# Start ticks of weight conversions in an FFT filter followed by two MLPs

## Chip, cores and metric

The kernel runs on one core of a Trainium2 chip. The metric is the device time of one execution in microseconds (us); a run is repeated, and the median counts.

## What is computed

```python
def _attn_ref(x, filt_r, filt_i):            # x: (2, 3008, 256)
    X = np.fft.rfft(x, axis=1)
    Y = X * (filt_r + 1j * filt_i)[None]
    return np.fft.irfft(Y, n=x.shape[1], axis=1)

def _moe_ref(x, w_in, w_out):                # x: (6016, 256), w_in: (256, 2048), w_out: (2048, 256)
    h = x @ w_in
    return np.maximum(0.01 * h, h) @ w_out

def _moe2_ref(x, w_in, w_out):
    r = np.maximum(x @ w_in, 0.0)
    return (r * r) @ w_out
```

The output is `_moe2_ref(_moe_ref(_attn_ref(x)))`, each MLP with weights of its own, all in float32.

## The kernel before, in words

The Fourier transform comes first, as products with small constant matrices on TensorE; it fills the first 130 us. Then come the two MLPs. Everything below is about them.

**Tiles and steps.** The 6016 tokens are cut into six macro tiles, 0 to 5, of 2 x 512 or (tiles 2 and 5) 2 x 480 tokens. The 2048 hidden units are cut into eight pairs of 128, p = 0 to 7. One step is one pair for one macro tile: 45 matmuls, 21 of them up (line 368, results `ph`, weights `wai` or `wbi`), 24 of them down (line 463, sums `py`, weights `wao` or `wbo`). The up product is a Strassen scheme: seven block products instead of eight, from blocks `b11`, `b21`, `b22` of the tile and from sums `t1` to `t4` of blocks. In the first MLP tile 0 is visited with pairs 0 to 3, then tile 1 with all pairs, then tile 0 again with pairs 4 to 7, then tiles 2 to 5; the second MLP visits tiles 0 to 5. That is 96 steps.

**Two-part numbers.** A float32 product is made of three matmuls of rounded parts: each operand is split into a rounded part `hi` (a ScalarE copy, line 338 for a tile, 269 for weights) and the rest `lo` (a subtraction on VectorE or GpSimd, line 344 for a tile, 273 for weights). The tile's seven operands are called `xop`; their sums `xs` are made at line 333 on GpSimd.

**Inside a step.** `up` (lines 408 to 449) has four parts. The first makes two products, and VectorE's `v` (line 402). The second makes three, of which the last adds into the buffer that `v` has read, and VectorE's `u` and an `h`. The third makes none. The fourth makes two, of which the first adds into the buffer that `u` has read, and two more `h`. For each of four results ScalarE makes `g` and `gp` (lines 381, 382), and GpSimd their difference (line 391). `down` (line 451) follows `up` of the next step, part by part. At the end of a tile `finish` copies the sums `py` out, on VectorE and ScalarE (lines 485 to 489).

**Ticks.** What is not part of a step is set by a clock that goes on by 8 ticks (`TM`) per step. `begin` puts the entries of a table (name of a piece of work: ticks from its start) on a list, and `tick` issues what is due. Engines take their instructions in the order in which they are issued, so the tables decide what stands ahead of what on each engine. A tick is 1.3 us where a step is 10.5 us. Tile 1 begins at tick 32, the second visit of tile 0 at 96, tiles 2 to 5 at 128, 192, 256 and 320, and the second MLP at 384. The preparation of a tile (`MACRO`) goes from 24 ticks before its beginning to 2 after it.

**Weights.** They arrive as 64-bit floats and are made into 32-bit ones by `narrow_w` (lines 193 to 257): ScalarE takes the absolute value (`size`, line 209), VectorE makes two passes (`upper`, lines 213 and 214), then one each for `signed` (217), `exp` (222) and `low` (228), and `add` (236) puts the parts together, first for half 0 (the up weights, `wi`), then for half 1 (the down weights, `wo`). `sums` (241 to 244) makes four more blocks on GpSimd. The first MLP's pairs 4 to 7 go through table `NARROW_1`, with start ticks `STARTS_1`, and are split at once. The second MLP's eight pairs go through `NARROW_2`, from tick `STARTS_2` on, one every 32 ticks, and are put to DRAM; `split_w` loads and splits them later (`SPLIT_W`, table start 8 ticks per pair, and `LATE`). The raw words are `wraw`, loaded on SyncE's queue; each load waits for `low` of the pair before. All other loads and stores are on SyncE's queue too.

The two tables as they stand:

```python
NARROW_2 = dict(
    size0=4, upper0=7, signed0=7, exp0=9, low0=10, load0=10, size1=10, add0=12, upper1=15, signed1=15, sums=16, exp1=16,
    low1=17, load1=17, add1=18, out_o=19, out_i=26,
)
MACRO = dict(
    load=-24, sum0=-16, sum1=-15, sum2=-12, hi_b11=-11, sum3=-9, hi_b21=-8, hi_t2=-8, lo_b11=-8, lo_t2=-8,
    hi_t1=-7, hi_t4=-7, lo_t1=-7, lo_b21=-6, hi_t3=-2, lo_t3=-1, lo_t4=0, hi_b22=1, lo_b22=2,
)
```

Of the kernel before, what the change touches and what calls it, by code (L numbers as in the profile page):

```python
# [30 lines left out]
NP = DFF // (2 * P)  # L31
TT = 512
NWA = 4
# [27 lines left out]

TM = 8
STARTS = (-10, 34, 72, 112)
STARTS_1 = (0, 16, 32, 56)
STARTS_2 = 80


HALF = 4
# [13 lines left out]
    low1=17, load1=17, add1=18, out_o=19, out_i=26,  # L82
)

LATE = 20
SPLIT_W = dict(load=16, hi_i=18, hi_o=19, lo_i=20, lo_o=23)
FIRST = dict(
    hi_t1=-13, hi_b11=-13, lo_t1=-13, lo_b11=-13, sum1=-12, hi_b21=-12, lo_b21=-11, hi_t2=-11, lo_t2=-10, sum2=-9,
# [14 lines left out]
    S=("lo_o",),  # L103
    M=("lo_b11", "lo_b21", "lo_t2", "lo_t3", "lo_t4"),
# [47 lines left out]
def fft_filter_then_two_mlps(  # L152
# [102 lines left out]
    def split_w(layer, p, kind, w):  # L255

        t = {}

        def load():
            for k, (n, tag) in enumerate(((7, "wi32"), (4, "wo32"))):  # L260
                w[k] = wt_p.tile([P, n, P], F32, tag=tag, name=tag, bufs=1)
                nc.sync.dma_start(w[k], w2_d[p][:, 7 * k : 7 + 4 * k])

        def hi(k):
            pool, tag = (wa_p, "wa") if p < NWA else (wb_p[0], "wb")
            n = (7, 4)[k]
            t[k] = pool.tile([P, 2, n, P], F32R, tag=tag + "io"[k], name=tag + "io"[k])
            (w_in, w_out)[k][layer, p] = t[k]
            nc.scalar.activation(t[k][:, 0], w[k], AF.Copy)

        def lo(k):
            eng = engine(kind, "lo_" + "io"[k])
            eng.tensor_tensor(t[k][:, 1], w[k], t[k][:, 0].bitcast(F32), ALU.subtract)

        return {
            "load": load, "hi_i": lambda: hi(0), "hi_o": lambda: hi(1), "lo_i": lambda: lo(0), "lo_o": lambda: lo(1),
        }

    def engine(kind, step):
        return nc.vector if step in ON_VECTOR[kind] else nc.gpsimd  # L280
# [4 lines left out]
    def begin(c, steps, table, start):  # L285

        due[c].extend((start + t, steps[name]) for name, t in table.items())
# [12 lines left out]
    NM = len(macros)  # L300
# [195 lines left out]
    with ExitStack() as fctx:  # L496
# [268 lines left out]
        for p in range(NWA, NP):  # L765
            begin("M", narrow_w(0, p, "N1"), NARROW_1, STARTS_1[p - NWA])
        for p in range(NP):
            begin("M", narrow_w(1, p, "N2"), NARROW_2, STARTS_2 + 4 * p * TM)
            begin("M", split_w(1, p, "S", {}), SPLIT_W, ((NM - 1) * NP + p) * TM + (LATE if p >= NWA - 1 else 0))
        for part in range(4):  # L770
            up(0, part)
        up(1, 0)
# [6 lines left out]
    for i in range(last):  # L779
        v, p = steps[i]  # L780
        l, m, _, p1 = visits[v]
        accs = dict(acc)
        if (i + 1) * TM == STARTS_2:
            for k in range(2):
# [64 lines left out]
```

## Time and profile before

| | |
|---|---|
| median of 3 runs | 1163.13 us (1162.51 to 1165.67) |
| profiled execution, its own time | 1165.77 us |
| its span | 1163.1 us |
| TensorE (PE) busy | 1117.3 us, 96% |
| weight loads (PEld) busy | 883.9 us |
| GpSimd (POOL) busy | 765.6 us, 66% |
| VectorE (DVE) busy | 652.8 us, 56% |
| ScalarE (ACT) busy | 649.8 us, 56% |
| TensorE's waits for VectorE's `u`, all | 15.7 us in 8 |
| TensorE's waits for VectorE's `v`, all | 11.6 us in 5 |
| GpSimd's subtraction for an activation (line 391) | 1318 ns on average, 384 of them |
| mean granted clock of TensorE | 0.993 |

How to read it: the span goes from the first to the last instruction of the profiled execution. PE, DVE, ACT, POOL and SP are TensorE, VectorE, ScalarE, GpSimd and SyncE. A row of the timeline gives an instruction's start and length, and in brackets the idle time of its engine just before it and what ended that. The granted clock is the share of full speed that TensorE was given.

### The profile page before, as it was taken

How to read it: one execution, taken by the hardware profiler on the slowest of the kernel's cores; microseconds unless marked ns; L12 is line 12 of the kernel's file. 1: busy time of each engine (PE TensorE's matmuls, PEld its weight loads, DVE VectorE, ACT ScalarE, POOL GpSimd, SP SyncE). 2: the span in 40 equal slices, each digit the busy share in tenths (PEclk: the TensorE clock that was granted, in tenths of full speed). 3: DMA queues.
4: the chain of work that ended last, by engine and by line, in shares of the span. 5: the costliest groups of instructions: out<-in, count | busy, mean ns of one | idle time of the engine just before them, and what ended most of it. 6: DMA issues, size and time to landing. Idle time of an engine off the chain costs nothing.

```text
span 1163.1 us, 14072 instructions
## 1 busy us (share of the span) xinstructions
PE 1117.3 (96%) x4800; PEld 883.9 (76%) x4800; DVE 652.8 (56%) x870; ACT 649.8 (56%) x1209; POOL 765.6 (66%) x616
## 2 busy tenths in 40 slices
PE   7899978999899899899899999999999999999998
PEld 3466866888688688678688788788888788788887
DVE  6899788565854854855744643533534434435432
ACT  3855456554554554555555765655656555656554
POOL 3785598777757857756767876745647547557544
PEclk9999999999999999999999999999999999999999
DMA  7653712116022022023032030010100200200100
GB/s 229 189 158 117 265 54 78 55 56 239 20 82 95 23 84 86 19 80 96 1 111 87 28 106 38 31 40 1 63 11 1 71 1 1 71 1 1 37 1 34
DMA packets 35238, 80.12 MB, mean 69 GB/s; under 512 B 4544, under 2 KB 14880, under 8 KB 35040
## 3 DMA queue, kind: packets, MB, share of 16 engines
q1 hardware_dynamic: 35168, 79.25, 20.6%
q8 instruction: 37, 0.61, 0.2%
q14 instruction: 33, 0.27, 0.1%
HBM read 51.31 MB, written 27.92 MB: 68 GB/s over the span
## 4 chain that ended last, share of the span: by engine, by line
PE 76%; DVE 10%; ACT 4%; issue 4%; POOL 3%; DMA 2%; SPq 0%; DVEq 0%; POOLq 0%; ACTq 0%
PE py L463 38%; PE ph L368 34%; DVE xop L344 3%; PE pi L629 1%; POOL gp L391 1%; ACT g L381 1%; PE pa L571 1%; PE px L583 1%; DMA xin<-in_x 1%; ACT xop L338 1%; DVE u L402 1%; DVE wm L213 1%; DVE wi L222 1%; PE zps L613 1%; ACT gp L382 1%
## 5 line engine op out<-in xcount | busy, mean ns | idle before, releaser
L391 POOL TENSOR_TENSOR gp<-g,gp 128x512 fp32r<-128x512 f32 (+1 forms) x384 | 502.6, 1318 | 340.0 <-ACT gp L382 102.4
L463 PE MATMUL py<-gp,wao 128*128 128x512 f32 (+1 forms) x1152 | 287.8, 391 | 0.3 <-POOL gp L391 0.3
L463 PE MATMUL py<-gp,wbo 128*128 128x512 f32 (+1 forms) x1152 | 288.0, 392 | 0.0
L368 PE MATMUL ph<-xop,wai 128*128 128x512 f32 (+1 forms) x1008 | 259.2, 394 | 20.5 <-DVE v L402 11.6
L368 PE MATMUL ph<-xop,wbi 128*128 128x512 f32 (+1 forms) x1008 | 254.9, 391 | 8.7 <-DVE u L402 8.7
L463 PEld LDWEIGHTS py<-gp,wbo 128*128 128x128 f32 x1152 | 217.2, 189 | 48.1 <-POOL gp L391 0.2
L463 PEld LDWEIGHTS py<-gp,wao 128*128 128x128 f32 x1152 | 216.5, 188 | 48.5 <-POOL gp L391 0.7
L368 PEld LDWEIGHTS ph<-xop,wai 128*128 128x128 f32 x1008 | 187.7, 188 | 69.3 <-DVE v L402 14.1
L368 PEld LDWEIGHTS ph<-xop,wbi 128*128 128x128 f32 x1008 | 187.5, 187 | 53.4 <-DVE u L402 10.4
L381 ACT ACTIVATE g<-h 128x512 f32<-128x512 f32 (+1 forms) x144 | 88.9, 617 | 133.5 <-DVE h L402 128.9
L402 DVE TENSOR_TENSOR u<-ph,p 128x512 f32<-128x512 f32 (+1 forms) x96 | 65.0, 677 | 156.4 <-PE ph L368 156.4
L402 DVE TENSOR_TENSOR v<-ph,p 128x512 f32<-128x512 f32 (+1 forms) x96 | 65.0, 677 | 136.8 <-PE ph L368 64.7
L389 ACT ACTIVATE g<-h 128x512 f32<-128x512 f32 (+1 forms) x144 | 89.0, 618 | 85.6 <-DVE h L398 84.1
L387 ACT ACTIVATE r<-ph 128x512 f32<-128x512 f32 (+1 forms) x48 | 28.2, 587 | 106.5 <-PE ph L368 106.5
L390 ACT ACTIVATE gp<-h 128x512 fp32r<-128x512 f32 (+1 forms) x144 | 87.4, 607 | 0.0
L382 ACT ACTIVATE gp<-h 128x512 fp32r<-128x512 f32 (+1 forms) x144 | 87.3, 607 | 0.0
L381 ACT ACTIVATE g<-ph 128x512 f32<-128x512 f32 (+1 forms) x48 | 28.2, 587 | 97.9 <-PE ph L368 97.9
L398 DVE CUSTOM_DVE_ANT_0 h<-ph,p 128x512 f32<-128x512 f32 (+1 forms) x48 | 32.6, 680 | 86.8 <-PE ph L368 86.8
L402 DVE TENSOR_TENSOR h<-ph,p 128x512 f32<-128x512 f32 (+1 forms) x48 | 32.7, 680 | 73.7 <-PE ph L368 73.7
L421 ACT ACTIVATE p<-ph 128x512 f32<-128x512 f32 (+1 forms) x96 | 54.7, 570 | 1.5 <-PE ph L368 1.5
L601 POOL TENSOR_TENSOR t<-xc,fi 128x384 f32<-128x384 f32 x32 | 35.8, 1121 | 21.1 <-ACT xc L591 16.5
L344 DVE TENSOR_TENSOR xop<-x,xop 128x512 fp32r<-128x512 f32 (+1 forms) x33 | 41.0, 1243 | 10.4 <-ACT xop L338 10.4
(200 smaller groups left out, 1146.3 us busy)
## 6 DMA issues: line engine op xcount, KB each, us to landing
wraw<-in_w SPq DMA_DIRECT2D x32, 512.0 KB
xin<-in_x SPq DMA_DIRECT2D x32, 160.0 KB
xt<-xo SPq DMA_DIRECT2D x26, 188.0 KB
yt<-o SPq DMA_DIRECT2D x16, 256.0 KB
x<-yt SPq DMA_DIRECT2D x4, 1024.0 KB
out<-o SPq DMA_DIRECT2D x16, 256.0 KB
w<-wi SPq DMA_DIRECT2D x8, 448.0 KB
wi<-w SPq DMA_DIRECT2D x8, 448.0 KB
```

The lines of the kernel that those rows point to most:

```text
L344: eng.tensor_tensor(t[:, 1, :n], x_f32[v][name], t[:, 0, :n].bitcast(F32), ALU.subtract)
L368: nc.tensor.matmul(ph[:, :n], w[:, i, k], x[:, j, :n], start=(first and a == 0), stop=(a == 2), skip_group_check=True)
L381: nc.scalar.activation(g[:, :n], h[:, :n], AF.Prelu, alpha=0.01)
L382: nc.scalar.activation(t[:, 0, :n], h[:, :n], AF.Prelu, alpha=0.01)
L389: nc.scalar.activation(g[:, :n], h[:, :n], AF.Square)
L390: nc.scalar.activation(t[:, 0, :n], h[:, :n], AF.Square)
L391: nc.gpsimd.tensor_tensor(t[:, 1, :n], g[:, :n], t[:, 0, :n].bitcast(F32), ALU.subtract)
L398: nc.vector._custom_dve(dve_ops.TENSOR_ADD_SAT, out=t[:, :n], in0=ph[:, :n], in1=s[:, :n], s0=F32_MAX, s1=0.0)
L402: nc.vector.tensor_tensor(t[:, :n], ph[:, :n], s[:, :n], ALU.add)
L421: nc.scalar.activation(p1[:, :n], ph[0][:, :n], AF.Copy)
L463: nc.tensor.matmul(acc[c, t][:, :n], w[:, j, 2 * f + c], g[:, k, :n], start=(p == p0 and f == t and a == 0), stop=(p == p1 - 1 and f != t ...
L601: nc.gpsimd.tensor_tensor(t2, xc, fi_of(units[s][1], units[s][1] + 1), ALU.mult)
```

## The change

Four numbers in tables are changed; no instruction is added or taken away.

```diff
-STARTS_1 = (0, 16, 32, 56)
-STARTS_2 = 80
+STARTS_1 = (0, 32, 48, 64)
+STARTS_2 = 96
...
-LATE = 20
+LATE = (12, 12, 12, 20, 20, 20, 20, 20)
...
-            begin("M", split_w(1, p, "S", {}), SPLIT_W, ((NM - 1) * NP + p) * TM + (LATE if p >= NWA - 1 else 0))
+            begin("M", split_w(1, p, "S", {}), SPLIT_W, ((NM - 1) * NP + p) * TM + LATE[p])
```

Pairs 5, 6 and 7 of the first MLP begin their conversion at ticks 32, 48 and 64. Pair p of the second MLP begins at 96 + 32p; the load of its first raw words goes with `STARTS_2` and is 16 ticks later too. The splits of pairs 0, 1 and 2 are 12 ticks later; those of 3 to 7 stay.

On VectorE at the beginning of tile 2 (`xop` are the tile's operands, `u`, `v` and `h` the additions of a step), before:

```order
L217 SCALAR_TENSOR_TENSOR wb__2736<-wraw_2386,wb__2736 128x512
L402 TENSOR_TENSOR v<-ph,p_2752 128x512
L344 TENSOR_TENSOR xop<-x,xop 128x480
L344 TENSOR_TENSOR xop<-xs,xop 128x480
L222 TENSOR_SCALAR wi_2770<-wb__2736 128x512
L344 TENSOR_TENSOR xop<-x,xop 128x480
L228 SCALAR_TENSOR_TENSOR wm<-wraw_2386,wi_2770 128x512
L402 TENSOR_TENSOR u<-ph,p_2752 128x512
```

and with the change:

```order
L402 TENSOR_TENSOR v<-ph,p_2745 128x512
L344 TENSOR_TENSOR xop<-x,xop 128x480
L344 TENSOR_TENSOR xop<-xs,xop 128x480
L344 TENSOR_TENSOR xop<-x,xop 128x480
L402 TENSOR_TENSOR u<-ph,p_2745 128x512
```

The passes of a weight conversion (lines 217, 222 and 228) have gone from between the tile's subtractions, and from ahead of `v`.

On GpSimd, from the preparation of tile 2 on (`gp` are the activations, `wi` and `wo` the weights of pair 0), with the change:

```order
L333 TENSOR_TENSOR xs<-x 128x480
L241 TENSOR_TENSOR wi_2551<-wi_2551 128x128
L242 TENSOR_TENSOR wi_2551<-wi_2551 128x128
L243 TENSOR_TENSOR wi_2551<-wi_2551 128x128
L244 TENSOR_TENSOR wi_2551<-wi_2551 128x128
L333 TENSOR_TENSOR xs<-x,xs 128x480
L391 TENSOR_TENSOR gp<-g,gp 128x512
L236 TENSOR_TENSOR wo_2660<-wb__2624,wm 128x512
L391 TENSOR_TENSOR gp<-g,gp 128x512
L333 TENSOR_TENSOR x<-x 128x480
L391 TENSOR_TENSOR gp<-g,gp 128x512 x2
L333 TENSOR_TENSOR xs<-x,xs 128x480
```

Before, the sums and the addition of pair 0 stood further ahead, and the first two `xs` followed one another. The sums of pair 1, which stood behind the tile's beginning, are a whole conversion later.

On SyncE's queue, at the second visit of tile 0 (`xop` are the tile's operands, loaded again; `wraw_2431` and `wraw_2433` the raw words of the second MLP's pair 0), with the change:

```order
L362 DMA xop<-xop_t_1320 128x1024
L362 DMA xop<-xop_t_1322 128x1024
L362 DMA xop<-xop_b_1324 128x1024
L362 DMA xop<-xop_t_1336 128x1024
L362 DMA xop<-xop_t_1348 128x1024
L188 DMA wraw_2431<-in_w 128x1024
L188 DMA wraw_2433<-in_w 128x1024
L362 DMA xop<-xop_b_1366 128x1024
```

Before, these two loads of raw words stood ahead of the first of these rows, and one of pair 1 behind it.

## Rows read from the trace of the kernel before

**Rows 1.** Timeline of TensorE: start, length, instruction, idle time before and its releaser.
```profile
172.57 2.92 PE L368 MATMUL ph<-xop,wai 128*128 128x512 f32 x6 [5.66 <-DVE u L402]
184.39 0.97 PE L368 MATMUL ph<-xop,wai 128*128 128x512 f32 x3 [2.78 <-DVE v L402]
...
306.40 1.69 PE L368 MATMUL ph<-xop,wbi 128*128 128x512 f32 x6 [2.00 <-DVE u L402]
315.81 1.05 PE L368 MATMUL ph<-xop,wai 128*128 128x480 f32 x3 [2.28 <-DVE v L402]
```
**Rows 2.** Busy time by stretch: length, five engines busy, PEclk, DMA share, GB/s.
```profile
158.53:191.50 32.97, 23.95 (x91) 17.85 (x90) 28.70 (x28) 15.77 (x30) 28.60 (x22) 0.90 0.10 32
191.50:202.00 10.50, 10.50 (x46) 8.45 (x45) 8.73 (x13) 6.88 (x14) 9.16 (x8) 1.00 0.43 152
296.52:323.65 27.13, 22.85 (x92) 17.78 (x91) 23.19 (x27) 13.21 (x26) 21.20 (x17) 0.94 0.15 49
383.18:408.78 25.60, 21.07 (x92) 16.41 (x91) 23.48 (x26) 13.14 (x27) 21.08 (x18) 1.00 0.14 46
471.80:497.95 26.15, 21.73 (x91) 16.46 (x90) 23.95 (x26) 13.46 (x27) 21.49 (x17) 1.00 0.14 45
560.97:586.67 25.70, 21.41 (x92) 16.48 (x91) 23.49 (x26) 13.21 (x27) 21.05 (x17) 1.00 0.02 6
646.06:667.38 21.32, 20.52 (x92) 16.49 (x91) 15.72 (x17) 15.70 (x30) 18.19 (x14) 1.00 0.12 35
730.39:751.89 21.50, 21.27 (x92) 16.82 (x91) 13.98 (x16) 14.91 (x29) 15.37 (x12) 1.00 0.00 1
```
**Rows 3.** Timeline of VectorE before tile 2 of the first MLP.
```profile
299.86 0.68 DVE L402 TENSOR_TENSOR v<-ph,p 128x512 f32<-128x512 f32 x1
...
303.06 1.52 DVE L222 TENSOR_SCALAR wi<-wb__2736 128x512 int32<-128x512 int32 x1
304.50 0.65 DVE L344 TENSOR_TENSOR xop<-x,xop 128x480 fp32r<-128x480 f32 x1
305.07 0.68 DVE L228 SCALAR_TENSOR_TENSOR wm<-wraw,wi 128x512 f32<-128x512 uint32 x1
305.68 0.68 DVE L402 TENSOR_TENSOR u<-ph,p 128x512 f32<-128x512 f32 x1
```
**Rows 4.** Timeline of VectorE before the first tile of the second MLP.
```profile
647.63 0.66 DVE L402 TENSOR_TENSOR v<-ph,p 128x480 f32<-128x480 f32 x1 [1.98 <-ACT p L421]
...
649.10 1.78 DVE L344 TENSOR_TENSOR xop<-xs,xop 128x512 fp32r<-128x512 f32 x1
650.80 1.78 DVE L344 TENSOR_TENSOR xop<-x,xop 128x512 fp32r<-128x512 f32 x1
652.51 0.64 DVE L402 TENSOR_TENSOR u<-ph,p 128x480 f32<-128x480 f32 x1
```
**Rows 5.** Busy time by stretch: transfers of tile 0, and four small sums on GpSimd.
```profile
264.00:266.00 2.00, 2.00 (x11) 1.59 (x10) 1.97 (x3) 2.00 (x5) 1.78 (x2) 1.00 1.01 410
314.00:316.73 2.73, 0.92 (x4) 0.78 (x5) 2.69 (x5) 0.66 (x2) 2.57 (x6) 0.95 0.00 0
```
**Rows 6.** Timeline of GpSimd: addition of half 1, and a tile's fourth sum.
```profile
319.70 1.28 POOL L236 TENSOR_TENSOR wo<-wb__2843,wm 128x512 f32<-128x512 f32 x1
...
648.58 1.75 POOL L333 TENSOR_TENSOR xs<-x,xs 128x512 f32<-128x512 f32 x1
```
**Rows 7.** Timeline of ScalarE before tile 1.
```profile
168.32 0.63 ACT L338 ACTIVATE xop<-xs 128x512 fp32r<-128x512 f32 x1 [4.57 <-POOL xs L333]
```
**Rows 8.** Timeline of VectorE: two of the four additions that write out tile 0.
```profile
326.45 1.28 DVE L485 TENSOR_TENSOR o<-py,o 128x512 f32<-128x512 f32 x2
```
**Rows 9.** Timeline of VectorE before tile 1: passes of pair 5.
```profile
165.39 1.78 DVE L217 SCALAR_TENSOR_TENSOR wb__1561<-wraw,wb__1561 128x512 int32<-128x512 int32 x1
167.20 1.37 DVE L222 TENSOR_SCALAR wi<-wb__1561 128x512 int32<-128x512 int32 x1
...
170.17 1.75 DVE L228 SCALAR_TENSOR_TENSOR wm<-wraw,wi 128x512 f32<-128x512 uint32 x1
```

## Prediction

> **What bounds the kernel now.** I read the page first: TensorE is busy for 1117.3 of 1163.1 us, the other three engines for 650 to 766 us. So a gain can only come from TensorE's gaps. The waits of TensorE and its timeline then show where the gaps lie. In the two MLPs nearly all of the waiting stands at the beginnings of five macro tiles, always as a pair: once for VectorE's `u` in the last step of the old tile, once for VectorE's `v` in the first step of the new one [rows 1]. Tile 1 of the first MLP has 5.66 and 2.78 us; tile 2 has 2.00 and 2.28 us, and tiles 3, 4 and 5 have a pair like that each.
>
> To price a pair with all that follows from it I took the two steps around each beginning from the table by stretch [rows 2]. An undisturbed step of 512 columns is 10.50 us for 45 matmuls, as the stretch from 191.50 shows. A step of 480 columns I take as 10.50 x 480/512 = 9.84, a mixed step (21 matmuls of the new tile, 24 of the old) as 10.19 where the new tile is the narrow one and 10.15 where the old one is. What two steps take above that is the price of a beginning:
> - tile 1: 32.97 - 21.00 = 11.97
> - tiles 2 to 5: 27.13 - 20.69 = 6.44; 25.60 - 19.99 = 5.61; 26.15 - 21.00 = 5.15; 25.70 - 20.69 = 5.01; together 22.2
> - first tile of the second MLP, where no conversion runs any more: 21.32 - 19.99 = 1.33; its second tile: 21.50 - 21.00 = 0.50
>
> So 34.2 us are lost at five beginnings that have a weight conversion beside them, against 0.5 to 1.3 where there is none. A part of the price is clock: the granted clock was 0.90 over the pair of tile 1 and 0.94 over that of tile 2, and 1.00 in the other pairs. Tile 1 lost 11.97 us, but its two waits are only 8.44.
>
> Why VectorE is late is to be seen in its timeline. At tile 2, between `v` at 299.86 and `u` at 305.68, it runs three subtractions of the macro tile and, in between, two passes of a weight conversion, 1.52 and 0.68 us [rows 3]. The wait that they end is 2.00 us. In the second MLP the same three subtractions stand between `v` at 647.63 and `u` at 652.51 with nothing else [rows 4], and TensorE doesn't wait for that `u`. The three alone just fit; each pass more is a wait. The same holds for the second wait: the first three passes over the other half of the weights lie ahead of `v`.
>
> **The change, part by part.** No operation is added or removed; tables of start ticks move them.
>
> *Second MLP's conversions, from 80 + 32p to 96 + 32p.* Pairs 1, 3, 5 and 7 began 16 ticks before tiles 2, 3, 4 and 5, so their VectorE passes at 7 to 17 ticks lay from 9 ticks before a beginning to 1 after it, where the tile's own subtractions are. Now they begin with the tile. Pairs 0, 2, 4 and 6 begin 32 ticks before a tile; their last VectorE passes are done 15 ticks ahead of it, and the tile's subtractions begin 8 ahead. The order of VectorE's instructions bears it out: `v`, three subtractions, `u`, and nothing between. So I expect each of the four beginnings to fall from 22.2/4 to something between the two free ones, 0.50 and 1.33. I take 0.9 since both are beginnings of the same kind and the next part adds work on GpSimd: 4 x 0.9 = 3.6 stays, **18.6 us are saved** (bounds: 16.9 and 20.2).
>
> *What arrives ahead of the tiles.* From 16 to 14 ticks ahead, GpSimd now has the four small sums (2.57 us busy [rows 5]) and one 512-column addition (1.28 us [rows 6]) between its subtractions for the tile: 3.85 us. At 1.3 us each, GpSimd does four subtractions for activations in a step of 10.5 us, 5.2 us, and in this one four for the tile, 5.2; 5.2 + 5.2 + 3.85 = 14.3, so it runs up to 3.8 us late into the next step, which has four for activations and one tile subtraction of some 1.75 [rows 6], 7.0, and so 3.5 us to spare. Late next is the fourth of the tile's sums, the `xs` for which ScalarE's rounding of it waits, and behind that ScalarE's `g`. At tile 1 ScalarE waited 4.57 us so [rows 7]. That wait is covered as long as VectorE's `h` comes after it, which it does in the rows of the second MLP. Below, this part costs nothing; above, all of 4.57 per tile, which is a rival. I take nothing beyond the 0.9.
>
> *What arrives behind the tiles.* Passes at 7 to 10 ticks now meet the writing out of the old tile at 4 to 8 ticks. For one tile that is two VectorE copies; for tile 2 it is four additions, two of them 1.28 us [rows 8]. Pair 6 of the first MLP stood so before the change, beginning with tile 1: its step from 191.50 took 10.50 us [rows 2], no loss. For tile 2 with twice as much I put 0.5 us; the bounds are 0 and 2.56.
>
> *First MLP's conversions, 16, 32, 56 to 32, 48, 64.* Pair 5 leaves the beginning of tile 1. Its passes between `v` and `u` there were 1.78 + 1.37 + 1.75 = 4.90 us [rows 9], of a wait of 5.66: 0.8 stays. The second wait, 2.78, had only passes of pair 5 ahead of `v` besides one subtraction of the tile; it goes. With a wait under 1 us I expect the clock to stay up as at tiles 3 to 5, where waits of 2 us left it at 1.00. With the 0.5 of a free beginning and some lateness from pair 4, which stays, 1.5 is left: **10.5 us are saved** (bounds 8 and 11.2). Pairs 5 to 7 now begin 16 ticks apart as 4, 5 and 6 did; pair 7 is ready at tick 88 and first used in that step.
>
> *Three splits 12 ticks later.* Split 2 now has its GpSimd pass right ahead of the first tile of the second MLP. Split 3 stands at that beginning already, which takes 1.33 against 0.50 for the one without; so a split costs up to 0.8 there and perhaps nothing, and I put 0.3 us for this one, which lies further ahead. They are needed from tick 384 on, and the last is done at 371, so nothing waits for them.
>
> *SyncE's queue.* The first two loads of the second MLP's weights, 1.05 MB, now lie between two of the seven `xop` loads, ahead of the last. At 410 GB/s [rows 5] that is 2.6 us for the last, which is needed in the last part of its step, some 7 us after the first. I put nothing; bounds 0 and 2.6.
>
> **Sum:** 18.6 + 10.5 - 0.5 - 0.3 = 28.3 us. The profiled execution took 1165.77 us (span 1163.1) and would come to 1137.5. The median of the runs is 1163.13, 2.6 lower, and what is taken away is the same in both: **1135 us**.
>
> **A rule against it.** Where GpSimd ran beside them, the tile's subtractions took 1.78 us each, next to a GpSimd subtraction of 1.75 [rows 4, 6]; with GpSimd idle the same took 0.65 [rows 3]. The Trainium skill (SBUF — State Buffer, section "SBUF: two separate sides") says why: a VectorE instruction with two inputs in SBUF and a GpSimd instruction that reads SBUF share a port pair as an exclusive lock, "the other fully blocks". The rows agree. By that rule a GpSimd that is made fuller ahead of a tile slows these subtractions further.
>
> **The rivals.**
> - *GpSimd never idle ahead of the tiles (0.15).* Each of the three subtractions then waits for one whole GpSimd instruction: 3 x (0.65 + 1.28) = 5.8 us between `v` and `u`, where the free beginning had 4.2 (from 648.29 to 652.51) [rows 3, 4, 6]. That is 1.6 us at each of four tiles, 6.4: **1141 us**. For it: 14.3 us of work for GpSimd in a step of 10.5. Against: the lateness is worked off before the tile begins.
> - *GpSimd's lateness reaches TensorE (0.09).* 4.57 us at each of four tiles, 18.3 of the 22.2; with 8 at tile 1 the gain is some 12 us: **1151 us**. Against: at tile 1 ScalarE's wait lay inside the wait for VectorE.
> - *Slower (0.03).* Tile 1 is the only beginning in the trace that had a conversion begun 32 ticks ahead, pair 4, and it is the dearest. If pair 4 and not pair 5 costs the 11.97, they stay, and four more tiles get the same: 4 x 11.97 - 22.2 = +25.7, **1189 us**. It decides from a price of 22.2/4 = 5.6 us per tile on. Against: pair 5's passes explain 4.90 of 5.66.
> - *Nothing moves (0.01).* The order of VectorE's instructions speaks against it.
>
> **How the numbers follow.** The forecast has 0.72, with 1131 to 1139 as its own range: 31.4 us are saved if every cost is at its lower bound (20.2 + 11.2). The range of 8 in 10 also takes in the first rival and reaches to 1146. No change means within 0.3%, some 3.5 us, about what a measurement can tell: 0.03. Slower 0.03, faster 0.94.
>
> **What would show it.** Right: the pairs of waits for `u` and `v` at tiles 2 to 5 gone, under 1.5 us each with what follows; tile 1's two steps near 22.5 us with the clock at 1.00. First rival: the waits for `u` stay at 1 to 2 us with three subtractions of over 1.8 us each. Second: ScalarE waits over 4 us for `xs`, and TensorE for `v` or a product's buffer behind it. I am wrong if new waits stand in the steps at 4 to 10 ticks behind a beginning, or if tile 1 still costs over 5 us.

## The result, and the profile after

The changed kernel takes 1136.2 us (median of 4 runs, 1134.99 to 1136.63), the kernel before 1163.14 in the runs beside it. The ratio is 0.9763, with a 95% interval of 0.9746 to 0.978. The forecast was 1135.0 with a range of 1131 to 1146.

The profiled execution took 1136.23 us, with a span of 1134.1 and a mean granted clock of 1.000 (0.993 before). Against the profiled execution of before that is 29.5 us less; 2.0 of these lie before the first matmul of the MLPs (at 130.93 us before, at 128.92 now), in a part that the change doesn't touch. From that matmul to the last one it is 26.95 us less, and that is what the medians show.

TensorE's waits in the changed kernel, all with their sum, number and longest:

```profile
PE ph L368 <- DVE u L402: 2.5, 5, 0.8
PE ph L368 <- POOL xop L344: 2.1, 5, 0.8
PE ph L368 <- DVE v L402: 1.3, 5, 0.4
```

The 15.7 and 11.6 us of waiting for `u` and `v` have become 2.5 and 1.3. Busy time by stretch of the changed kernel, with the columns of [rows 2]: the two steps around the beginnings of tiles 1 and 2, the two steps behind that of tile 2, the beginnings of tiles 3, 4 and 5, and that of the second MLP.

```profile
156.53:178.93 22.40, 21.60 (x91) 16.52 (x90) 13.53 (x17) 14.11 (x28) 21.63 (x16) 1.00 0.00 0
...
284.47:305.19 20.72, 20.72 (x91) 16.90 (x90) 14.05 (x17) 13.08 (x26) 17.78 (x14) 1.00 0.10 36
305.19:326.63 21.44, 20.58 (x91) 16.51 (x90) 18.73 (x23) 9.84 (x20) 14.83 (x14) 1.00 0.28 98
366.37:387.06 20.69, 20.57 (x91) 16.56 (x90) 14.35 (x17) 13.04 (x26) 18.37 (x14) 1.00 0.09 35
450.62:471.69 21.07, 21.07 (x92) 16.82 (x91) 14.47 (x17) 13.39 (x27) 18.51 (x14) 1.00 0.09 34
535.24:555.96 20.72, 20.72 (x92) 16.91 (x91) 14.07 (x17) 13.10 (x27) 17.80 (x14) 1.00 0.09 36
616.17:638.13 21.96, 20.79 (x92) 16.48 (x91) 16.34 (x17) 15.71 (x30) 20.19 (x15) 1.00 0.11 35
```

Against the undisturbed times of the prediction, tile 1 has 22.40 - 21.00 = 1.40 us left of 11.97. Tiles 2 to 5 have 0.03, 0.70, 0.07 and 0.03 left of 22.2 together [rows 2]. VectorE is busy for 14 us in the stretches of tiles 2 to 5 instead of 23 to 24, GpSimd for 18 instead of 21. What left them stands elsewhere: the stretch behind tile 2 has 18.73 us of VectorE and takes 21.44 us for two narrow steps (two undisturbed ones are 19.8 in the trace), 1.6 too many.

VectorE before tile 2 now, to be held against [rows 3]:

```profile
286.12 0.69 DVE L402 TENSOR_TENSOR v<-ph,p 128x512 f32<-128x512 f32 x1 [2.11 <-PE ph L368]
286.73 0.84 DVE L344 TENSOR_TENSOR xop<-x,xop 128x480 fp32r<-128x480 f32 x1
287.50 1.75 DVE L344 TENSOR_TENSOR xop<-xs,xop 128x480 fp32r<-128x480 f32 x1
289.17 1.75 DVE L344 TENSOR_TENSOR xop<-x,xop 128x480 fp32r<-128x480 f32 x1
290.84 0.68 DVE L402 TENSOR_TENSOR u<-ph,p 128x512 f32<-128x512 f32 x1
```

`v` now has to wait for TensorE, not TensorE for `v`, and `u` comes 4.03 us after the end of `v`, about as at the free beginning of the second MLP [rows 4].

That VectorE itself was late before, and not an engine ahead of it, can be read from the kernel before. At tile 2 no row of VectorE from `v` to `u` has idle time before it [rows 3], and this is its queue ahead of the second `v`, with no idle time behind the first row:

```profile
310.30 1.17 DVE L344 TENSOR_TENSOR xop<-x,xop 128x480 fp32r<-128x480 f32 x1 [1.25 <-ACT xop L338]
311.39 1.51 DVE L213 TENSOR_SCALAR wm<-wm 128x512 f32<-128x512 f32 x1
312.94 1.38 DVE L214 TENSOR_SCALAR wb__2843<-wm 128x512 int32<-128x512 int32 x1
314.36 0.83 DVE L217 SCALAR_TENSOR_TENSOR wb__2843<-wraw,wb__2843 128x512 int32<-128x512 int32 x1
315.11 0.65 DVE L402 TENSOR_TENSOR v<-ph,p 128x480 f32<-128x480 f32 x1
```

ScalarE's copies `p`, which the two `v` read, were there 1.8 and 3.8 us earlier:

```profile
297.51 0.58 ACT L421 ACTIVATE p<-ph 128x512 f32<-128x512 f32 x1
310.81 0.55 ACT L421 ACTIVATE p<-ph 128x480 f32<-128x480 f32 x1
```

So ScalarE's part of a conversion (`size`) is not what held up these `v`; no run moves it alone.

ScalarE ahead of tile 2 in the changed kernel:

```profile
292.03 0.60 ACT L338 ACTIVATE xop<-xs 128x480 fp32r<-128x480 f32 x1 [3.27 <-POOL xs L333]
```

GpSimd's lateness is there, as the prediction said: ScalarE waits for `xs` 21.2 us in 7 waits over the kernel, 6.0 in 7 before. At tiles 2 to 5 these waits are 3.27 to 3.96 us, and the beginnings there still have only 0.03 to 0.70 us left.

### The profile page after: what moved, and what is told of

Read it like the earlier page. It is cut to its first block, busy times and chain, and to the rows that moved or that the text cites. A ratio compares the mean times of both kernels' runs of the same rounds, so it can differ in the third digit from the quotient of the medians.

```text
span 1134.1 us, 14074 instructions
## 1 busy us (share of the span) xinstructions
PE 1110.9 (98%) x4800; PEld 879.6 (78%) x4800; DVE 646.6 (57%) x870; ACT 649.4 (57%) x1209; POOL 762.6 (67%) x616
## 4 chain that ended last, share of the span: by engine, by line
PE 82%; DVE 9%; issue 3%; POOL 2%; ACT 2%; DMA 2%; SPq 0%; DVEq 0%; POOLq 0%; ACTq 0%
PE py L463 41%; PE ph L368 36%; DVE xop L344 1%; PE pa L571 1%; PE px L583 1%; DMA xin<-in_x 1%; PE zps L613 1%; DVE h L402 1%; DVE wm L213 1%; POOL gp L391 1%; DMA x<-xt 1%; PE pi L629 1%; DVE zin L622 1%; DVE bin L578 1%; DVE v L402 1%
## 5 line engine op out<-in xcount | busy, mean ns | idle before, releaser
L344 DVE TENSOR_TENSOR xop<-x,xop 128x512 fp32r<-128x512 f32 (+1 forms) x33 | 47.1, 1428 | 10.5 <-ACT xop L338 6.8
L601 POOL TENSOR_TENSOR t<-xc,fi 128x384 f32<-128x384 f32 x32 | 36.1, 1133 | 21.4 <-ACT xc L591 15.8
```

The lines of the kernel that those rows point to most:

```text
L344: eng.tensor_tensor(t[:, 1, :n], x_f32[v][name], t[:, 0, :n].bitcast(F32), ALU.subtract)
L601: nc.gpsimd.tensor_tensor(t2, xc, fi_of(units[s][1], units[s][1] + 1), ALU.mult)
```

## The experiments

Prices of beginnings below are worked out as in the prediction, from the table by stretch. Where the schedule and the clock are the same, TensorE's steps come out alike to about 0.02 us from one kernel to the next, so single profiles tell small terms apart; the medians are given with them. Three places are exceptions, which differ between profiles without a change of theirs: the first two steps (17.1 or 16.6 us together), the step ahead of tile 1 with the new `STARTS_1` (11.87 or 11.25), and one step at the last tile of the second MLP (10.60 or 10.88).

### One part alone

The second MLP's part without the first MLP's:

```diff
-STARTS_1 = (0, 32, 48, 64)
+STARTS_1 = (0, 16, 32, 56)
```

> The change without its first row: the second MLP's conversions at 96 + 32p and the later splits, the first MLP's still at 0, 16, 32, 56. Theory A (VectorE's passes of a conversion between and ahead of a tile's subtractions make the waits, so each place is worth its own price): tiles 2 to 5 lose 0 to 1 us each in the two steps around their beginnings instead of 6.4, 5.6, 5.2 and 5.0, tile 1 keeps its 12 us; 17 to 20 us under the kernel before, some 1145 us. Theory B (GpSimd's work of a conversion makes them): the same here for tiles 2 to 5, so this run only shares out the gain; if the shares of this run and of the next don't add up to the 27 us of the whole change, there is a third cause.

Measured: 1147.61 us beside 1162.57, ratio 0.9864 (0.9847 to 0.9881), 15 us less. Tiles 1 and 2 in its table by stretch:

```profile
157.48:190.49 33.01, 23.62 (x91) 17.60 (x90) 28.74 (x28) 15.80 (x30) 28.65 (x22) 0.90 0.09 32
296.04:316.77 20.73, 20.73 (x91) 16.91 (x90) 14.06 (x17) 13.09 (x26) 17.79 (x14) 1.00 0.09 36
```

Tile 1 keeps its 12.0 us, with the clock at 0.90; tile 2 is free. From the first matmul of the MLPs to the last it has 16.6 us less than the kernel before. That is under the 17 to 20 that I expected: the beginnings became as cheap as I put them, but the expectation left out over 4 us that are lost in other steps, as in the changed kernel.

The first MLP's part alone, on the kernel before:

```diff
-STARTS_1 = (0, 16, 32, 56)
+STARTS_1 = (0, 32, 48, 64)
```

> The kernel before with the first MLP's conversions at 0, 32, 48, 64 and nothing else changed. Theory A: tile 1 falls from 12.0 to about 1.4 us over its two steps, the other tiles keep their prices; 10 to 11 us under the kernel before, some 1152.5 us. The rival by which pair 4, which began 32 ticks ahead and stays, costs the 12 us: no gain, 1163 us.

Measured: 1152.11 us beside 1162.57, ratio 0.9902 (0.9884 to 0.992), 10.5 us less. Tiles 1 and 2:

```profile
156.10:178.49 22.39, 21.58 (x91) 16.46 (x90) 13.51 (x17) 14.12 (x28) 21.63 (x16) 1.00 0.00 0
283.51:310.64 27.13, 22.82 (x91) 17.76 (x90) 23.55 (x27) 13.21 (x26) 21.25 (x17) 0.94 0.15 49
```

The parts add up: 16.6 + 10.5 = 27.1 us by the steps, 26.95 together. The rival by which pair 4 costs tile 1 its 12 us is refuted, since pair 4 is where it was.

### Later still, and at the old place again

```diff
-STARTS_2 = 96
+STARTS_2 = 112
-LATE = (12, 12, 12, 20, 20, 20, 20, 20)
+LATE = (28, 28, 28, 28, 28, 28, 28, 28)
```

> The changed kernel with the second MLP's conversions 16 ticks later still, at 112 + 32p, so that pairs 0, 2, 4 and 6 begin 16 ticks ahead of tiles 2, 3, 4 and 5; all splits at 28 ticks, behind the last conversion. Theory A: it is the place that counts and not that they are later: the waits for u and v come back at tiles 2 to 5, 5 to 6.5 us each, 18 to 23 us over the changed kernel, 1154 to 1159 us; tile 1 stays at 1.4. A rival by which starting later is what helps (raw words there in time, less beside the first visits): no slower than the changed kernel, 1136 us. The splits now lie across the beginning of the second MLP and may cost 1 to 2 us there.

Measured: 1154.89 us, ratio 0.9931 (0.9917 to 0.9946) to the kernel before, so 18.7 us over the changed kernel (20.4 by the steps of the MLPs). Tiles 2 to 5 and the second MLP's beginning:

```profile
282.40:308.06 25.66, 21.39 (x92) 16.48 (x90) 23.59 (x27) 13.10 (x26) 21.00 (x17) 1.00 0.13 47
367.59:394.31 26.72, 22.17 (x92) 17.72 (x90) 23.41 (x26) 13.16 (x26) 21.42 (x18) 0.94 0.14 49
457.32:483.47 26.15, 23.28 (x92) 17.61 (x90) 23.95 (x26) 13.60 (x27) 21.49 (x17) 0.93 0.13 46
546.47:572.16 25.69, 22.95 (x91) 17.62 (x90) 23.49 (x26) 13.30 (x27) 21.05 (x17) 0.93 0.13 46
631.70:657.03 25.33, 22.14 (x91) 17.90 (x90) 18.41 (x18) 17.13 (x32) 22.36 (x16) 0.93 0.21 58
```

The prices are back: 4.97, 6.73, 5.15 and 5.00, 21.9 us (22.2 before the change), though now other pairs stand there. It is the place that counts, not that the work is later. The splits that now lie across the second MLP's beginning cost 3.4 us there (25.33 against 21.96, with the clock at 0.93), more than the 1 to 2 I had put.

### GpSimd's part away from the beginnings

```diff
-    ... add0=12, ... sums=16, ... add1=18, out_o=19, out_i=26,
+    ... add0=20, sums=21, add1=23, out_i=26, out_o=27,
```

(on the kernel before)

> The kernel before with the start ticks as they were, but in the second MLP's conversions GpSimd's part is taken away from the tiles' beginnings: the first addition at 20 instead of 12 ticks, the four sums at 21 instead of 16, the second addition at 23 instead of 18, so 4, 5 and 7 ticks behind a beginning instead of 4 ahead to 2 behind. VectorE's passes stay where they were. Theory A: the waits stay, 1160 to 1163 us (the few us at most come from VectorE passes that GpSimd no longer holds up). Theory B: they go, 1141 to 1146 us. If the port that both share makes the passes long, in between, with passes and subtractions nearer to 0.7 than to 1.7 us.

Measured: 1157.5 us beside 1162.57, ratio 0.9957 (0.9942 to 0.9972), 5.1 us less. TensorE's waits at tiles 2 to 5, in its timeline:

```profile
302.62 1.70 PE L368 MATMUL ph<-xop,wbi 128*128 128x512 f32 x6 [2.02 <-DVE u L402]
311.06 0.93 PE L368 MATMUL ph<-xop,wai 128*128 128x480 f32 x3 [1.31 <-DVE v L402]
315.19 1.67 PE L368 MATMUL ph<-xop,wai 128*128 128x480 f32 x6 [0.40 <-DVE u L402]
...
387.44 2.77 PE L368 MATMUL ph<-xop,wbi 128*128 128x480 f32 x6 [2.42 <-DVE u L402]
475.31 2.33 PE L368 MATMUL ph<-xop,wbi 128*128 128x512 f32 x6 [2.25 <-DVE u L402]
563.16 1.70 PE L368 MATMUL ph<-xop,wbi 128*128 128x512 f32 x6 [2.02 <-DVE u L402]
571.48 0.92 PE L368 MATMUL ph<-xop,wai 128*128 128x480 f32 x3 [1.19 <-DVE v L402]
```

The waits for `u` are what they were, 2.02 to 2.42 us. Those for `v` fall from 2.1 to 2.3 us to 1.31 and 1.19 and, at tiles 3 and 4, to nothing. VectorE's passes ahead of that `v` are shorter where GpSimd doesn't run; at tile 3 two of the three are these (1.32 and 0.82 us before):

```profile
394.22 0.43 DVE L214 TENSOR_SCALAR wb__3582<-wm 128x512 int32<-128x512 int32 x1
394.68 0.69 DVE L217 SCALAR_TENSOR_TENSOR wb__3582<-wraw,wb__3582 128x512 int32<-128x512 int32 x1
```

So GpSimd's part had a share of a fifth at most (4.2 of the 22.2 us by the steps), by way of VectorE's passes. This is the branch of the expectation that lies in between; Theory B as the whole cause is refuted. The share is read too high for three reasons. Of the 4.2 us, 1.4 are the lower clock that tile 2 had behind its wait for `v` before and doesn't have here. At tiles 2 and 5, compared with beginnings at a clock of 1.00 (25.66 us for tile 2 in the kernel with the passes 16 ticks ahead again, 25.70 for tile 5 before), only 0.3 and 0.4 us are gained although the wait for `v` is 1 us shorter, since a new wait for `u` of 0.4 us follows it. At tiles 3 and 4 (0.9 and 1.1 us gained) a part of the relief may also come from the slower matmuls behind the wait for `u` there (2.77 and 2.33 us for six, 1.70 elsewhere), which give VectorE time; the two shares aren't told apart.

### The splits alone

```diff
-LATE = 20
+LATE = (12, 12, 12, 20, 20, 20, 20, 20)
...
-            begin("M", split_w(1, p, "S", {}), SPLIT_W, ((NM - 1) * NP + p) * TM + (LATE if p >= NWA - 1 else 0))
+            begin("M", split_w(1, p, "S", {}), SPLIT_W, ((NM - 1) * NP + p) * TM + LATE[p])
```

(on the kernel before)

> The kernel before with nothing changed but the splits of pairs 0, 1 and 2, which are 12 ticks later. Theory A: the pairs of waits at tiles 1 to 5 stay as they were, and the two steps around the beginning of the second MLP get the 0.6 us that the changed kernel has more there; about 1163.5 us. If the splits had a part in the gain, tile 5's beginning would get cheaper.

Measured: 1163.3 us (one run; 1162.95 beside it). The step ahead of the second MLP takes 10.55 us instead of 9.93, the 0.6 us that the changed kernel has there too. Tile 5's two steps sum up as before. The splits have no part in the gain. By the tables they had to move since pair 7's conversion now lies at ticks 320 to 346, where the first split stood; no run tries the change without it.

### GpSimd's part nearer to the tile

```diff
-    ... sums=16, ... add1=18, out_o=19, out_i=26,
+    ... sums=22, add1=23, out_i=26, out_o=27,
```

(on the changed kernel)

> The changed kernel with GpSimd's last part of a second-MLP conversion moved from 16 and 18 to 22 and 23 ticks: for pairs 0, 2, 4 and 6 that is 10 and 9 ticks ahead of tiles 2 to 5, right in front of the tile's own GpSimd work. Rival of the prediction (GpSimd's lateness reaches TensorE): ScalarE's wait for xs grows from 3 to over 4 us and 1 to 4 us per tile appear on TensorE, 1140 to 1150 us. If GpSimd's lateness is covered by the slack of a step, as the forecast had it: within 2 us of the changed kernel.

Measured: 1136.69 us, ratio 0.978 (0.976 to 0.9801), the changed kernel's 0.9763 (0.9746 to 0.978). In the table by stretch tile 3, the dearest of the four, is at

```profile
369.52:390.38 20.86, 20.54 (x91) 16.59 (x90) 11.62 (x17) 13.52 (x27) 20.02 (x18) 1.00 0.09 35
```

against 20.69 in the changed kernel. GpSimd is busy for 20.02 of 20.86 us there, and still only 0.2 us reach TensorE. But this asks little more than the changed kernel does: ScalarE's waits for `xs` at tiles 2 to 5 grew by only 0.2 to 0.4 us, to 3.60 to 4.18. The rival of the prediction by which GpSimd's lateness costs 4.57 us per tile is refuted for waits of this length; none longer at those tiles was tried.

### Two passes less between v and u

```diff
-    size0=4, upper0=7, signed0=7, exp0=9, low0=10, load0=10, size1=10, ...
+    size0=4, upper0=7, signed0=7, size1=10, exp0=11, low0=11, load0=11, ...
```

(on the kernel before)

> The kernel before with two VectorE passes of a second-MLP conversion (exp and low of half 0) at 11 ticks instead of 9 and 10; at tiles 2 to 5 that moves them from between v and u to just behind u. The passes ahead of v stay. Theory A: the waits for u at tiles 2 to 5 (2.00, 2.41, 2.25, 2.02 us) go and those for v (2.28, 2.12, 2.17, 2.28) stay: 8 to 10 us under the kernel before, 1153 to 1155 us. If the two waits of a pair have one common cause, both go or both stay: 1141 to 1145 or 1163 us.

Measured: 1163.62 us beside 1162.95, ratio 1.0005 (0.9995 to 1.0016): no difference. TensorE's waits at tile 2, and VectorE's third subtraction between `v` and `u`:

```profile
305.38 1.69 PE L368 MATMUL ph<-xop,wbi 128*128 128x512 f32 x6 [1.08 <-DVE u L402]
314.79 0.92 PE L368 MATMUL ph<-xop,wai 128*128 128x480 f32 x3 [2.28 <-DVE v L402]
```
```profile
302.98 1.74 DVE L344 TENSOR_TENSOR xop<-x,xop 128x480 fp32r<-128x480 f32 x1
```

My expectation failed. The two passes were 1.52 + 0.68 = 2.20 us [rows 3], but the wait for `u` fell only by 0.92. The third subtraction now runs beside GpSimd and takes 1.74 us instead of 0.65, which eats 1.09 of it. So the shares of a wait can't be read off the lengths of the passes that stand before it. The step ahead of each tile is 0.94 us shorter, 3.8 us for four; 2.6 of that are lost at tiles 3 and 4, where the granted clock fell behind the wait for `v` this time, and 0.6 in the step from 264.34, where `v` is late.

### The passes earlier within their steps

Three kernels on the base of the kernel before: half 0's passes at 3 and 4 ticks, half 1's at 11 and 12, and both.

```diff
-    size0=4, upper0=7, signed0=7, exp0=9, low0=10, load0=10, size1=10, add0=12, upper1=15, signed1=15, sums=16, exp1=16,
-    low1=17, load1=17, add1=18, out_o=19, out_i=26,
+    size0=2, upper0=3, signed0=3, exp0=4, low0=4, load0=5, size1=10, upper1=11, signed1=11, exp1=12, low1=12, add0=12,
+    load1=13, sums=16, add1=18, out_o=19, out_i=26,
```

(this is both; half 0 alone has the new ticks of the steps that end in 0, half 1 alone those that end in 1)

> The kernel before with VectorE's five passes over half 0 of a second-MLP conversion at 3 and 4 ticks instead of 7 to 10, so that none of them is ahead of v or between v and u in the last step before tiles 2 to 5; half 1 and GpSimd's part stay. The run before this one took only the two passes between v and u away, and the waits for u fell from 2.0 to 2.4 us to 1.1 to 1.5 and not to nothing. Theory A, mended (all that is queued on VectorE from the passes ahead of v on counts for u): the waits for u at tiles 2 to 5 go altogether, those for v stay at 2.1 to 2.3 us; 10 us less in the steps ahead of the tiles, 1152 to 1154 us, or up to 1158 where a lower clock follows the waits for v. If something other than the passes makes v and u late there: under 5 us less, over 1158 us.

> The same with half 1 instead of half 0: its five passes at 11 and 12 ticks instead of 15 to 17, which puts all five just behind u in the last step before tiles 2 to 5, where two h and one subtraction of the tile follow, and then v. Theory A as the prediction put it (the passes right ahead of v make the wait for v): the waits for v go, 9 to 12 us less, 1151 to 1154 us. Theory A, mended (all that is queued on VectorE counts, and five passes of 1.0 to 1.7 us are more than the three that stood ahead of v): the waits for v stay or grow to 2 to 4 us, 1163 to 1170 us.

> Both halves earlier as in the two runs above, start ticks as before the change. Theory A as the prediction put it: both waits go at tiles 2 to 5, 22 us less, 1140 to 1143 us. Theory A, mended: the waits for u go; between u and the next v VectorE now has five passes of some 6 us where the changed kernel had 2.7 us idle and 1.1 us to spare, so the waits for v stay at 1.5 to 2.5 us: 1152 to 1156 us.

Measured: 1164.72 us beside 1162.47 for half 0, ratio 1.0013 (1.0002 to 1.0025); 1171.15 for half 1, 1.0075 (1.0054 to 1.0097); 1175.09 for both, 1.0102 (1.0084 to 1.012). None of these became faster. Half 1 alone came out where the mended theory had it, a little over its 1170, but the waits are other ones than it says: TensorE waits 10.6 us for ScalarE's `p` in 8 waits, and for `v` only once. For the other two both theories had a gain, and fell; for half 0 the number lies where I had put that something other than the passes makes `v` and `u` late, but the rows show that it is the passes again, now ahead of `h`. With half 0 earlier, TensorE at tile 2 and ScalarE ahead of it:

```profile
295.66 1.69 PE L368 MATMUL ph<-xop,wbi 128*128 128x512 f32 x6 [0.72 <-ACT p L421]
301.08 1.70 PE L368 MATMUL ph<-xop,wbi 128*128 128x512 f32 x6 [0.92 <-DVE u L402]
...
310.49 0.98 PE L368 MATMUL ph<-xop,wai 128*128 128x480 f32 x3 [2.28 <-DVE v L402]
```
```profile
292.94 0.63 ACT L381 ACTIVATE g<-h 128x512 f32<-128x512 f32 x1 [3.89 <-DVE h L402]
...
295.04 0.57 ACT L421 ACTIVATE p<-ph 128x512 f32<-128x512 f32 x1
```

Five passes behind `u` hold up the two `h` of that step. ScalarE waits 3.89 us for the first, works off four activations and only then makes `p`, the copy for which TensorE waits (0.72 us), and `v` after it; the three subtractions then make `u` late after all (0.92 us). The step takes 12.73 us, 12.81 before the change: the lateness went round by ScalarE and came back. With half 1 earlier it shows in steps without any tile work, too:

```profile
265.65 1.69 PE L368 MATMUL ph<-xop,wbi 128*128 128x512 f32 x6 [0.85 <-ACT p L421]
```

That step takes 11.64 us, and three more like it have 1.1 to 1.2 us too many. With half 0 earlier the like steps have 0.2 to 0.4 too many. So five passes in one place, ahead of two `h`, cost more than the table's own split, three ahead of `v` and two ahead of `u`, which in the kernel before costs 0 to 0.15 us where no tile is prepared. These three kernels therefore don't test the finer theory cleanly: they bring a wait of their own.

### Two kernels that might be better

```diff
-    M=("lo_b11", "lo_b21", "lo_t2", "lo_t3", "lo_t4"),
+    M=("lo_b11", "lo_b21", "lo_t2", "lo_t3", "lo_t4", "lo_b22"),
```

(on the changed kernel)

> The changed kernel with the subtraction for the tile's operand b22 on VectorE instead of GpSimd. It is what TensorE still waits for in the first step of a tile (GpSimd's xop, 2.1 us in 5 waits). If those waits are GpSimd's lateness alone they go: 2 to 3 us under the changed kernel, 1133 to 1134.5 us. If VectorE, which has this one pass more between v and u, is then late for u: no gain or up to 1 us more.

Measured: 1132.14 us beside 1162.95 (median of 5 runs, 1129.07 to 1133.05), ratio 0.9731 (0.9714 to 0.9749). That clearly beats the kernel before. The chip and the runs beside it are others than those of the changed kernel, so the ratios are to be compared; their intervals just touch, and the steps have to decide. Of TensorE's waits in the MLPs only these are left; the one for GpSimd's `xop` is gone:

```profile
PE ph L368 <- DVE u L402: 1.9, 4, 0.8
...
PE ph L368 <- DVE v L402: 1.3, 5, 0.4
```

By the steps it saves 0.4 to 0.8 us at each beginning of the second MLP's tiles, 3.3 us there. Another 1.2 us at the start of the MLPs and ahead of tile 1 are not its doing: the kernel with GpSimd's part nearer to the tile, which leaves `b22` alone, has them too. Of the 3.3, 0.3 lie in the step that comes out at 10.60 or 10.88 anyway. So the move is worth 3.0 to 3.3 us.

The same with the table of both halves earlier:

> The changed kernel with b22's subtraction on VectorE, which gave 1132.1 us, and with the table of both halves earlier: with starts at and 32 ticks ahead of a tile its passes at 3, 4, 11 and 12 ticks stand clear of the tile's subtractions and of most of the writing out at 4 to 8 ticks, where the changed kernel still loses 1.1 and 0.5 us behind tile 2 and 0.4 behind others. Mended theory: 0 to 3 us under 1132.1. If five passes in one place are too many beside the writing out: 0 to 4 us above it.

Measured: 1146.35 us, ratio 0.9854 (0.9836 to 0.9872), 14 us over the kernel above it, with TensorE waiting 8.7 us for `p` in 10 waits, as in the three kernels before, and 4.3 us in 4 for ScalarE's copies that write out a tile. The expectation was made before their cause was known, and fell with it.

## Why the prediction was right, and where it was off

- **Where the time is.** Right: the five beginnings cost 34.2 us and cost 2.2 now. One part undone or put back gives or takes what the table by stretch says, to a few tenths (16.6 + 10.5 against 26.95; 21.9 of 22.2 back at 16 ticks ahead).
- **Tiles 2 to 5.** Forecast 18.6 us with 20.2 as the upper bound; measured 21.4. The step "each falls to something between the two free ones, 0.50 and 1.33" was too careful: three of them are at 0.03 to 0.07. The two beginnings that I took as bounds aren't free. They have a wait for GpSimd's `xop` (0.23 to 0.81 us), which went when that subtraction was moved to VectorE, and which the first MLP's tiles don't show.
- **Tile 1.** Forecast 10.5, measured 10.57, with 1.40 left; the clock stayed at 1.00, as put. In two later profiles, with nothing changed there, 0.8 is left.
- **What arrives behind the tiles.** Forecast 0.5 us, all at tile 2; measured 1.65 at tile 2, 0.5 each at tiles 3 and 4 and 0.1 at tile 5, another 0.7 in a later step of tile 5, with the passes over half 1 of pair 7, and 0.7 in steps ahead of the tiles; 4 us in all. The prediction priced the step where passes meet the writing out of the old tile; there it is 1.5 us at the four tiles. Another 2.1 lie one step further, with the passes over half 1, where it put nothing: one undisturbed step (pair 6 at tile 1) stood for all. Why these passes cost something there and almost nothing in other steps wasn't tried.
- **The splits.** Forecast 0.3, measured 0.6.
- **SyncE's queue.** Put at nothing, with 2.6 us as a bound; the first step of tile 0's second visit takes 10.50 us (10.52 before), so nothing is lost.
- **The sum** of 28.3 was near to 26.95 since two errors nearly cancelled: one gain was 2.8 us larger than put, the small losses together 4 us larger (0.3 of them in the step that comes out at 10.60 or 10.88). That the total came so near is luck; the mechanism is not.
- **Why VectorE is late.** In the main right: the passes at the beginning, not GpSimd alone and not the splits. But "each pass more is a wait", with the 4.90 of 5.66 us at tile 1 as its sum, was too simple. Taking two passes of 2.20 us away shortened a wait by 0.92, and passes put at another place of the same step came back as lateness of `h`, `p` and `v`. What the whole change does, and these don't, is to take a conversion out of the steps that have a tile's work as well. That it is the place is shown by runs; that it is VectorE's passes is read from the rows, with GpSimd's part and the splits tested apart, and how a beginning's price divides among the passes stays open.
- **The rivals.** GpSimd's lateness is there (21.2 us of ScalarE's waiting for `xs`) and is covered, even with a little more of it. For the first rival, the three subtractions had to take 5.8 us from `v` to `u`, each meeting a whole GpSimd instruction; at tile 2 they took 4.0, and the first of them 0.84. Where GpSimd's work comes to lie beside such a subtraction, the price does show: 0.65 us became 1.74 in the run without the two passes. Pair 4 as the cause of tile 1's 12 us is refuted by the run with the first MLP's part alone.

## What to carry to other kernels

Where a bound engine's waits come in a regular pattern, price each place by the time of its steps against an undisturbed step, not by the waits: what follows a wait (a lower clock, the next wait) is in it, and the prices added up to 0.2 us here. Side work, like these conversions, that fits in every step but those that carry other side work should be moved out of those steps whole. Moved within a step it only made another result late here, by way of engines that wait for each other in turn. And look at what stays at a place that you call free before you make it a bound.

## What was not expected of the hardware

The same wait is followed by a lower granted clock at one place and not at another, and the place changes from kernel to kernel. In the kernel before, the pair at tile 2 had 0.94 and those at tiles 3 to 5 had 1.00 [rows 2]; with the splits alone changed, which leaves these steps as they are, it fell at all four tiles: at tile 2 as before, at tiles 3 to 5 in the first step of the pair (0.91, 0.90 and 0.88). The two steps of tile 3 read

```profile
380.77:394.59 13.82, 11.41 (x46) 9.05 (x45) 12.23 (x14) 8.46 (x18) 9.69 (x8) 0.91 0.12 38
394.59:406.37 11.78, 11.19 (x46) 8.54 (x45) 11.27 (x13) 4.78 (x10) 11.38 (x11) 0.96 0.17 53
```

and in the kernel before

```profile
383.18:395.88 12.70, 10.29 (x46) 8.19 (x45) 11.78 (x13) 7.34 (x16) 8.58 (x7) 1.00 0.13 41
395.88:408.78 12.90, 10.78 (x47) 8.22 (x46) 11.70 (x13) 5.79 (x13) 12.50 (x12) 1.00 0.15 50
```

Both pairs are 25.60 us long. Where the clock falls behind the wait for `u`, that step is 1.1 us longer (11.41 us of matmuls instead of 10.29), but VectorE catches up in that time: the wait for `v` falls from 2.12 to 0.59 us, and the next step is shorter by as much. Where it falls behind the wait for `v`, nothing catches up: tile 2 before the change paid 1.4 us more than its like (14.32 for the second step, 12.87 in the kernel that has the passes 16 ticks ahead again). What decides where it falls wasn't tried.
